# First attention step of a sigmoid-attention plus ReLU² feed-forward kernel: half of its scores moved to two-part products, its first queries loaded and multiplied in halves, three warm-up matmuls fewer

## The chip, the cores and the metric

One core of a Trainium2 chip runs the whole program. The metric is device time in microseconds (us), the median of a few runs; lower is better. The engines are PE (TensorE, with PEld for its weight loads), DVE (VectorE), ACT (ScalarE), POOL (GpSimd) and SP (SyncE, which here only issues transfers). ACT issues transfers too, on a queue of its own.

## The reference, cut to what matters

```
q, k, v: 8 batches x 12 heads x 448 x 64, fp32
attn = sigmoid(q @ k^T / sqrt(64) - log(448))
x    = (attn @ v), heads side by side: 3584 tokens x 768
h    = max(x @ w_in, 0)                # 768 -> 2048
out  = (s * h * h + b) @ w_out         # 2048 -> 768
```

The change touches only the first few microseconds of the attention.

## The kernel before, in words

The heads are worked through four at a time: one *step* takes a tile `qk` of 128 partitions x [2 pairs][queries, keys][448] (two pairs of heads; in a pair, one head lies on partitions 0 to 63 and the other on 64 to 127). There are 24 steps (8 batches x 3), and after them comes the feed-forward part, which is nearly four fifths of the time. The order of all instructions is the order in which the code is written (`manual_schedule`), so each engine works through its list in that order.

A step (the loop `for n, (b, t) in enumerate(quads)`, L584 to L611):

- `scores` (L397): for pair `i` and chunk `c` of 128 keys, both heads' scores go into one bank tile `psc` of 128 x 2 x 448. Steps 1 to 23 (`TWO`, L53) multiply *two parts*: each operand is split as a high part `qkh` rounded to fp32r (a copy) and the rest `qkl` (a subtraction), and three fp32r products (L413) stand for one fp32 product. Step 0 multiplies the raw fp32 operands (L419); one such instruction appears in the trace as two records, so a chunk of step 0 (two heads) is 4 records, a chunk of the other steps 6.
- the scores run through `sigmoid` (L392, on ACT) into a tile `a`; a chunk's bank is free again once its sigmoid is done. Score banks come from a pool of 3 (`ps_qk`); the chunk (0, 2) uses the bank tile of the products with `v` (`ps_av`) instead. In step 0 the warm-up tile `idle` takes the first of the three, so the chunks (0, 0), (0, 1), (1, 0), (1, 1), (1, 2) and the last keys' chunk go round the three banks, and the last keys' chunk waits for the sigmoid of (1, 0).
- `scores_last` (L429): the last 64 keys of both pairs (`psc_l`, L434); that of step n + 1 is run inside step n.
- `parts_hi` (L382, ACT) and `parts_lo` (L388, DVE) split the next step's operands.
- `attn_v` (L440, L445) and `attn_v_last` (L451, L454) multiply with `v` into `pav`; `store_x` (L459) copies the result out and stores it.
- between these, `ticks` runs jobs that prepare the feed-forward weights: raw 64-bit weights are fetched into `st` and converted by DVE and ACT (L204 to L220).

Ahead of the loop: step 0's `qk` tile is loaded in five transfers on two queues (L363 to L367), then step 1's tile as one transfer (L369), `v` of step 0 (L374), two weight tiles `st` (L493) and more, all on SP. PE runs `WARM` matmuls of zeros (L472) until the data are there. ACT loads its table (L467) and makes a small constant `e_bias`, which DVE then overwrites (L468).

In what follows (i, c) is the chunk c of pair i in step 0.

Of the kernel before, what the change touches and what calls it, by code (L numbers as in the profile page):

```python
# [34 lines left out]


TB = 512
WARM = 13
PARTS = ((0, 0), (0, 1), (1, 0))
AHEAD = 6  # L40
PIECES = (2, 1, 1, 2, 1, 1, 2, 1, 1, 2, 1, 1, 2, 1, 1, 2, 1, 1, 2, 1, 2, 1)
# [9 lines left out]
}  # L51
ROLL = 7
TWO = range(1, 24)  # L53

# [40 lines left out]
def sigmoid_attention_relu2_ffn(  # L95
# [10 lines left out]
    nc = tc.nc  # L106
    B, NQ, P, _, _, S = qk.shape
# [44 lines left out]
    first = ExitStack()  # L152
# [23 lines left out]
    def f32(ap):  # L176
        return ap.bitcast(F32)
# [4 lines left out]
    def sub(o, x, y):  # L182
        nc.vector.tensor_tensor(o, x, y, op=ALU.subtract)  # L183
# [170 lines left out]
    ps_av = pool(at, "ps_av", 1, space=PSUM, side="right")  # L354

    half = (slice(0, D), slice(D, P))
    quads = [(b, t) for b in range(B) for t in range(NQ)]
    NL = len(quads)

    def load(b, t, first=False):  # L360
        x = ld.tile([P, 2, 2, S], F32, tag="qk", name=f"qk_{b}_{t}")
        if first:
            nc.sync.dma_start(x[:, 0, 1, :P], qk[b, t][:, 0, 1, :P])  # L363
            nc.scalar.dma_start(x[:, 0, 0], qk[b, t][:, 0, 0])
            nc.sync.dma_start(x[:, 0, 1, P:], qk[b, t][:, 0, 1, P:])
            nc.scalar.dma_start(x[:, 1, 0], qk[b, t][:, 1, 0])
            nc.sync.dma_start(x[:, 1, 1], qk[b, t][:, 1, 1])  # L367
        else:
            nc.sync.dma_start(x, qk[b, t])  # L369
        return [x]  # L370
# [8 lines left out]
    def flat(x):  # L379
        return x.rearrange("p i x s -> p i (x s)")[:, :, :NX]  # L380

    def parts_hi(b, t, ld_):  # L382

        hi, lo = (hl.tile([P, 2, NX], F32R, tag=h, name=f"qk{h}_{b}_{t}") for h in "hl")
        nc.scalar.copy(hi, flat(ld_[0]))
        ld_.append((hi, lo))

    def parts_lo(ld_):  # L388
        hi, lo = ld_[-1]
        sub(lo, flat(ld_[0]), f32(hi))  # L390

    def sigmoid(psc, name):  # L392
        a = ap_.tile([P, 2, S], F32, tag="a", name=f"a_{name}")
        nc.scalar.activation(a, psc[:, :, :S], AF.Sigmoid, bias=nls, scale=SCALE)  # L394
        return a

    def scores(b, t, ld_):  # L397
        x = ld_[0]
        two = ld_.pop() if len(ld_) > 2 else None
        a = {}  # L400
        psc = {}
        order = [(i, c) for i in range(2) for c in range(3)]
        if two:
            order[2:4] = order[3], order[2]
        for i, c in order:

            pl, tag = (ps_av, "pav") if (i, c) == (0, 2) else (ps_qk, "psc")
            o = psc[i, c] = pl.tile([P, 2, 512], F32, tag=tag, name=f"psc_{b}_{t}_{i}_{c}")
            if two:
                cols = slice(S + c * P, S + (c + 1) * P)  # L410
                for m, (wi, xi) in enumerate(PARTS):
                    for j, r in enumerate(half):
                        nc.tensor.matmul(  # L413
                            o[:, j, :S], two[wi][r, i, cols], two[xi][r, i, :S],
                            start=m == 0, stop=m == 2,
                        )
            else:
                for j, r in enumerate(half):
                    nc.tensor.matmul(  # L419
                        o[:, j, :S], x[r, i, 1, c * P : (c + 1) * P], x[r, i, 0, :],  # L420
                        start=True, stop=True,
                    )
            if two and i + c == 1 and i:
                continue
            for k in [(i, c)] + [(1, 0)] * (two is not None and (i, c) == (0, 2)):
                a[k] = sigmoid(psc[k], f"{b}_{t}_{k[0]}_{k[1]}")
        return a

# [35 lines left out]
    loaded = {0: load(*quads[0], first=True)}  # L464
# [18 lines left out]
    def ticks(n, part):  # L483
        for _, _, fn in sorted(plan.pop((n, part), ()), key=lambda x: x[:2]):
            fn()
# [96 lines left out]
    at_step(NL - 1, "DVE", 1, lambda: base(0, 0, w1[0]))  # L582

    for n, (b, t) in enumerate(quads):  # L584
        ticks(n, "DVE")
        a = scores(b, t, loaded[n])
        if n == 0:
            al = scores_last(b, t, loaded[0])
        if n + 1 in TWO:
            parts_hi(*quads[n + 1], loaded[n + 1])  # L590
        ticks(n, "ACT")
        if n + 2 < NL:
            loaded[n + 2] = load(*quads[n + 2])
        ticks(n, "SP")
        for fn in stores:
            fn()
        stores.clear()
        if n == NL - 1:
            qkx.close()
            ps_h = pool(blk_ps, "ps_h", 2, space=PSUM)  # L600
        pav = attn_v(b, t, loaded[n], a)
        last = al
        if n + 1 < NL:
            al = scores_last(*quads[n + 1], loaded[n + 1])
        attn_v_last(loaded[n], last, pav)
        if n + 1 in TWO:
            parts_lo(loaded[n + 1])
        ticks(n, "END")
        store_x(b, t, pav)
        if n + 2 < NL:  # L610
            load_v(*quads[n + 2], loaded[n + 2])  # L611
# [142 lines left out]
    start = [(0, 0), (2, 0), (2, 1), (2, 2), (0, 2), (0, 1), (1, 1), (1, 2), (1, 0)]  # L754
# [4 lines left out]
    for i, f in enumerate(order):  # L759
# [17 lines left out]
        j, stage = divmod(i - LATE_AT, LATE_FOR)  # L777
# [152 lines left out]
    for n, blocks in enumerate(threes):  # L930
# [128 lines left out]
        for u, (i, p) in enumerate(L1):  # L1059
# [10 lines left out]
            for j in range(2):  # L1070
                m = 0
                for c in range(KC):
                    for wi, xi in PARTS:
                        nc.tensor.matmul(  # L1074
                            bk[:, j], wt[:, j, wi, c * P : (c + 1) * P], opd[i][xi][:, c, :],
                            start=i == ch[0] and m == 0,
                            stop=m == 3 * KC - 1,
# [111 lines left out]
        for j, (i, p) in enumerate(L2):  # L1189
# [8 lines left out]
            for e, tk in LAST if end else [(e, slice(TB)) for e in range(KC)]:  # L1198
                o = bk[:, e]
                if end:  # L1200
                    o = ps.tile([P, 2, TB], F32, tag="b", name=f"o_{e}_{tk.start}")[:, 0, tk]
                for f in range(2):
                    for m, (wi, gi) in enumerate(PARTS):
# [3 lines left out]
                            stop=p == NPP - 1 and f == 1 and m == 2,  # L1207
# [61 lines left out]
```

## Time and profile before

| | |
|---|---|
| median of 3 runs | 1039.72 us (1039.62 to 1039.72) |
| the profiled execution's own time | 1039.4 us |
| its span | 1037.5 us |
| PE busy in the span | 1033.5 us |
| DVE, ACT busy | 832.7 us, 618.3 us |
| instructions | 13890 |

The profiled execution takes 1.9 us more than its span (start and end lie outside it). The page of the profile gives busy times, the chain of work that ended last and the costliest groups of instructions; the trace behind it can be asked for every instruction in order of time, for who waited for whom, and for transfers with their time from issue to landing. A PE record's duration reaches over the next record's start, since matmuls are pipelined; how fast PE goes is read from the distance between starts.

### The profile page before, as it was taken

The page shows a single profiled execution, that of the slowest core. Times are in us where ns is not written, and L with a number is a line of the kernel's source. Part 1 is how long each engine was busy: PE and PEld are TensorE (multiplying, and loading weights), DVE is VectorE, ACT ScalarE, POOL GpSimd, SP SyncE. Part 2 cuts the span into 40 slices and gives each one's busy share as a digit, 9 for nine tenths or more (in the row PEclk, how much of TensorE's full clock was granted, in tenths as well). Part 3 has the DMA queues.
Part 4 walks back from the last instruction along what each step waited for, and adds up shares of the span by engine and source line. Part 5 has one row for each costly group of instructions (what it writes and reads, how often), then busy time and mean ns, then how long its engine had stood idle before and what let it go on. Part 6 is the DMA issues. An engine that isn't in the chain of part 4 may idle for free.

```text
span 1037.5 us, 13890 instructions
## 1 busy us (share of the span) xinstructions
PE 1033.5 (100%) x5287; PEld 780.6 (75%) x5287; DVE 832.7 (80%) x900; ACT 618.3 (60%) x667; POOL 0.2 (0%) x4
## 2 busy tenths in 40 slices
PE   9999999999999999999999999999999999999998
PEld 4545555555888888888888888888888888888887
DVE  4999999995988965898898897796455789888777
ACT  7999999988776755574445344344445335552432
POOL 0000000000000000000000000000000000000000
PEclk9999999999999999999999999999999999999999
DMA  8788989995999999999686676897666666676763
GB/s 325 273 333 337 354 325 395 344 397 193 333 364 367 357 408 410 342 342 320 201 269 190 217 229 220 290 318 249 197 192 194 194 193 195 192 228 217 221 228 118
DMA packets 101569, 287.16 MB, mean 277 GB/s; under 512 B 10241, under 2 KB 20353, under 8 KB 101505
## 3 DMA queue, kind: packets, MB, share of 16 engines
q1 hardware_dynamic: 101216, 285.84, 79.2%
q8 instruction: 42, 0.69, 0.3%
q10 hardware_dynamic: 288, 0.46, 0.1%
q14 instruction: 23, 0.18, 0.0%
HBM read 198.18 MB, written 88.08 MB: 276 GB/s over the span
## 4 chain that ended last, share of the span: by engine, by line
PE 100%; DVE 0%; issue 0%
PE o L1204 31%; PE h L1074 31%; PE pav L445 11%; PE psc L413 9%; PE ph L553 6%; PE po L744 6%; PE psc_l L434 2%; PE pav L454 2%; PE psc L419 1%; PE idle L472 0%; DVE C_t L183 0%; DVE zero L165 0%; DVE nls L166 0%
## 5 line engine op out<-in xcount | busy, mean ns | idle before, releaser
L1074 PE MATMUL h<-s_1h,wu 128*128 128x512 f32 x480 | 148.0, 389 | 0.0
L1074 PE MATMUL h<-s_0h,wu 128*128 128x512 f32 x480 | 147.8, 389 | 0.0
L394 ACT ACTIVATE a<-psc,nls 128x896 f32<-128x896 f32 x144 | 132.7, 1009 | 12.9 <-PE psc L413 10.2
L445 PE MATMUL pav<-a,v 128*64 128x448 f32 x576 | 113.5, 543 | 0.0
L1074 PEld LDWEIGHTS h<-s_1h,wu 128*128 128x128 f32 x480 | 90.1, 188 | 18.8
L1074 PEld LDWEIGHTS h<-s_0h,wu 128*128 128x128 f32 x480 | 90.1, 188 | 18.6
L947 ACT COPY G<-h 128x1024 f32<-128x1024 f32 x48 | 48.9, 1018 | 85.0 <-PE h L1074 58.0
L839 ACT ACTIVATE G<-G,b_sb,s_sb 128x1024 f32<-128x1024 f32 x48 | 59.8, 1245 | 61.4 <-DVE G L836 60.7
L1074 PE MATMUL h<-s_0l,wu 128*128 128x512 f32 x240 | 93.4, 389 | 0.0
L1074 PE MATMUL h<-s_1l,wu 128*128 128x512 f32 x240 | 93.4, 389 | 0.0
L445 PEld LDWEIGHTS pav<-a,v 128*64 128x64 f32 x576 | 39.2, 137 | 64.0 <-issue 44.8
L180 DVE TENSOR_TENSOR G<-G,h 128x1024 f32<-128x1024 f32 x40 | 48.7, 1219 | 39.0 <-PE h L1074 38.9
L1204 PE MATMUL o<-g_3h,wu 128*128 128x512 f32 (+1 forms) x244 | 79.0, 385 | 0.0
L1204 PE MATMUL o<-g_0h,wu 128*128 128x512 f32 x240 | 78.8, 389 | 0.0
L1204 PE MATMUL o<-g_1h,wu 128*128 128x512 f32 x240 | 78.8, 389 | 0.0
L1204 PE MATMUL o<-g_2h,wu 128*128 128x512 f32 x240 | 78.8, 389 | 0.0
L744 PE MATMUL po<-g,w 128*128 128x512 f32 x288 | 67.7, 389 | 0.0
L744 PEld LDWEIGHTS po<-g,w 128*128 128x128 f32 x288 | 54.1, 188 | 11.2
L553 PE MATMUL ph<-x0h,w 128*128 128x512 f32 x192 | 61.7, 390 | 0.0
L413 PE MATMUL psc<-qkh 64*128 64x448 f32 x276 | 53.0, 380 | 0.0
L1204 PEld LDWEIGHTS o<-g_3h,wu 128*128 128x128 f32 x244 | 45.7, 188 | 9.3
L1074 PEld LDWEIGHTS h<-s_0l,wu 128*128 128x128 f32 x240 | 45.0, 188 | 9.4
(152 smaller groups left out, 2025.4 us busy)
## 6 DMA issues: line engine op xcount, KB each, us to landing
wu<-wd SPq DMA_DIRECT2D x240, 512.0 KB, 4.3
wd<-t SPq DMA_DIRECT2D x36, 768.0 KB, 8.0
qk<-qk_t SPq DMA_DIRECT2D x23, 896.0 KB, 7.2
st<-w_out SPq DMA_DIRECT2D x16, 768.0 KB, 9.3
st<-w_in SPq DMA_DIRECT2D x16, 768.0 KB, 9.5
wd<-w SPq DMA_DIRECT2D x16, 768.0 KB, 5.8
v<-v_t SPq DMA_DIRECT2D x24, 448.0 KB, 5.6
xd<-xo SPq DMA_DIRECT2D x24, 448.0 KB, 4.3
```

The source lines that it names most:

```text
L180: nc.vector.tensor_tensor(o, x, y, op=ALU.add)
L394: nc.scalar.activation(a, psc[:, :, :S], AF.Sigmoid, bias=nls, scale=SCALE)
L413: nc.tensor.matmul(o[:, j, :S], two[wi][r, i, cols], two[xi][r, i, :S], start=m == 0, stop=m == 2,)
L434: nc.tensor.matmul(psc[half[i], j, :S], x[r, i, 1, 3 * P :], x[r, i, 0, :], start=True, stop=True,)
L445: nc.tensor.matmul(pav[r, i, :S], ld_[1][:, 3 * i + c, j, :], a[i, c][:, j, :], start=c == 0, stop=False,)
L454: nc.tensor.matmul(pav[r, i, :S], ld_[1][half[i], 6, j, :], a[half[i], j, :], start=False, stop=True,)
L553: nc.tensor.matmul(ph, w[:, k, wi, kc * P : (kc + 1) * P], x0[h][xi][:, cc, :], start=m == 0, stop=m == 3 * NCC - 1,)
L744: nc.tensor.matmul(pos[e], w[:, k, wi, kc * P : (kc + 1) * P], g[:, gi, :], start=first and i == 0, stop=last and i == 2,)
L839: nc.scalar.activation(x, x, AF.Identity, bias=b_sb, scale=s_sb)
L947: nc.scalar.copy(g(m, h), bk)
L1074: nc.tensor.matmul(bk[:, j], wt[:, j, wi, c * P : (c + 1) * P], opd[i][xi][:, c, :], start=i == ch[0] and m == 0, stop=m == 3 * KC - 1, sk ...
L1204: nc.tensor.matmul(o, wt[:, f, wi, e * P : (e + 1) * P], g[gi][:, f, tk], start=(end or i == ch[0] and p == 0) and f == 0 and m == 0, stop ...
```

## The change

Five things change, all but the last in step 0:

1. `WARM` goes from 13 to 10.
2. The first loads change queues: keys of (0, 0) and the remaining keys of pair 0 go to ACT's queue, the queries of pair 0 to SP's queue in two halves of 224 columns, and the queries of pair 1 stay on ACT's queue, now third there.
3. Chunk (0, 0) is multiplied by halves of the queries (224 columns, four instructions in place of two).
4. Pair 1 of step 0 is multiplied in two parts like the other steps; its parts are made by DVE alone: a copy (`qkh`) and a subtraction (`qkl`) of 128 x 832, ahead of step 0's other DVE jobs.
5. `TWO` is gone: every step has parts. Step 0 keeps its order of chunks.

```diff
-WARM = 13
+WARM = 10
...
+    cols2 = (slice(0, S // 2), slice(S // 2, S))
...
         if first:
-            nc.sync.dma_start(x[:, 0, 1, :P], qk[b, t][:, 0, 1, :P])
-            nc.scalar.dma_start(x[:, 0, 0], qk[b, t][:, 0, 0])
-            nc.sync.dma_start(x[:, 0, 1, P:], qk[b, t][:, 0, 1, P:])
+            nc.scalar.dma_start(x[:, 0, 1, :P], qk[b, t][:, 0, 1, :P])
+            for h in cols2:
+                nc.sync.dma_start(x[:, 0, 0, h], qk[b, t][:, 0, 0, h])
+            nc.scalar.dma_start(x[:, 0, 1, P:], qk[b, t][:, 0, 1, P:])
             nc.scalar.dma_start(x[:, 1, 0], qk[b, t][:, 1, 0])
             nc.sync.dma_start(x[:, 1, 1], qk[b, t][:, 1, 1])
...
-    def parts_hi(b, t, ld_):
+    def parts_hi(n, pairs=slice(0, 2)):
 
+        ld_ = loaded[n]
+        b, t = quads[n]
         hi, lo = (hl.tile([P, 2, NX], F32R, tag=h, name=f"qk{h}_{b}_{t}") for h in "hl")
-        nc.scalar.copy(hi, flat(ld_[0]))
+        copy = nc.scalar.copy if n else nc.vector.tensor_copy
+        copy(hi[:, pairs], flat(ld_[0])[:, pairs])
         ld_.append((hi, lo))
 
-    def parts_lo(ld_):
+    def parts_lo(n, pairs=slice(0, 2)):
+        ld_ = loaded[n]
         hi, lo = ld_[-1]
-        sub(lo, flat(ld_[0]), f32(hi))
+        sub(lo[:, pairs], flat(ld_[0])[:, pairs], f32(hi[:, pairs]))
...
-            if two:
+            if i or not first:
                 cols = slice(S + c * P, S + (c + 1) * P)
...
             else:
-                for j, r in enumerate(half):
-                    nc.tensor.matmul(
-                        o[:, j, :S], x[r, i, 1, c * P : (c + 1) * P], x[r, i, 0, :],
-                        start=True, stop=True,
-                    )
...
+                for s_ in cols2 if (i, c) == (0, 0) else (slice(0, S),):
+                    for j, r in enumerate(half):
+                        nc.tensor.matmul(
+                            o[:, j, s_], x[r, i, 1, c * P : (c + 1) * P], x[r, i, 0, s_],
+                            start=True, stop=True,
+                        )
...
     for n, (b, t) in enumerate(quads):
+        if n == 0:
+            parts_hi(0, slice(1, 2))
+            parts_lo(0, slice(1, 2))
         ticks(n, "DVE")
-        a = scores(b, t, loaded[n])
+        a = scores(b, t, loaded[n], first=n == 0)
```

PE's list where the warm-up ends, before (`psc_0_0_0` is the bank tile of chunk (0, 0), `psc_0_1_0` that of (1, 0); `qk_0` is step 0's tile, a name DMAHW is a transfer's signal):

```order
L472 MATMUL idle<-zero 128x256
L419 MATMUL psc_0_0_0_192<-qk_0_156 128x448 [waits DMAHW1_49,DMAHW0_49]
L419 MATMUL psc_0_0_0_192<-qk_0_156 128x448
L419 MATMUL psc_0_0_1_197<-qk_0_156 128x448 [waits DMAHW2_49]
L419 MATMUL psc_0_0_1_197<-qk_0_156 128x448
L419 MATMUL psc_0_0_2_202<-qk_0_156 128x448 x2
L419 MATMUL psc_0_1_0_207<-qk_0_156 128x448 [waits DMAHW4_49,DMAHW3_49,PE_49]
L419 MATMUL psc_0_1_0_207<-qk_0_156 128x448
L419 MATMUL psc_0_1_1_212<-qk_0_156 128x448 [waits Activation_49]
```

and the same place of the changed kernel:

```order
L479 MATMUL idle<-zero 128x256
L426 MATMUL psc_0_0_0_194<-qk_0_156 128x224 [waits DMAHW1_49,DMAHW0_49]
L426 MATMUL psc_0_0_0_194<-qk_0_156 128x224
L426 MATMUL psc_0_0_0_194<-qk_0_156 128x224 [waits DMAHW3_49]
L426 MATMUL psc_0_0_0_194<-qk_0_156 128x224
L426 MATMUL psc_0_0_1_201<-qk_0_156 128x448 [waits DMAHW2_49]
L426 MATMUL psc_0_0_1_201<-qk_0_156 128x448
L426 MATMUL psc_0_0_2_206<-qk_0_156 128x448 x2
L418 MATMUL psc_0_1_0_211<-qkh_0_188 128x448 [waits DVE_49,PE_49]
L418 MATMUL psc_0_1_0_211<-qkh_0_188 128x448
L418 MATMUL psc_0_1_0_211<-qkl_0_189,qkh_0_188 128x448 [waits DVE_49]
L418 MATMUL psc_0_1_0_211<-qkl_0_189,qkh_0_188 128x448
```

Chunk (0, 0) now waits for two transfers first and for a third half way, and chunk (1, 0) waits for DVE in place of the transfers.

DVE's list at the start of the changed kernel (`st` are raw weights, `qkl_1` is the low part for step 1):

```order
L475 MEMSET e_bias 128x1 [waits Activation_49]
L389 CAST qkh_0_188<-qk_0_156 128x832 [waits DMAHW5_49,DMAHW4_49]
L182 TENSOR_TENSOR qkl_0_189<-qk_0_156,qkh_0_188 128x832 [waits DVE_49]
L203 TENSOR_SCALAR wf_0_105<-st_0_180 128x768 [waits DMAHW0_49]
L203 TENSOR_SCALAR wf_8_107<-st_8_182 128x768 [waits DMAHW1_49]
L182 TENSOR_TENSOR qkl_1_246<-qk_1_163,qkh_1_245 128x1664 [waits DMAHW6_49,PE_49,Activation_49]
```

The second and third row are new; the others follow each other there as before. Behind step 0 no engine's list changes. On SP the first `v` and step 1's tile keep their places (fourth and fifth issue); since eight signals go round the transfers and there is one transfer more, the first `st` fetch now waits for the landing of the first keys, and the second for that of the first half of the queries.

## Rows read from the trace of the kernel before

**Rows 1.** The page: busy times, and the chain that ended last by engine

```profile
PE 1033.5 (100%) x5287; PEld 780.6 (75%) x5287; DVE 832.7 (80%) x900; ACT 618.3 (60%) x667; POOL 0.2 (0%) x4
...
PE 100%; DVE 0%; issue 0%
```

**Rows 2.** Chain that ended last, in order of time: start us, us, what

```profile
1.05 2.95 PE idle L472 x13
4.00 5.64 PE psc L419 x24
9.64 0.94 PE psc_l L434 x8
10.58 4.66 PE pav L445 x24
15.24 0.91 PE psc_l L434 x8
...
16.91 3.90 PE psc L413 x36
...
27.14 3.84 PE psc L413 x36
...
37.33 3.84 PE psc L413 x36
```

**Rows 3.** PE in order of time, 3 to 11 us: start, busy, what

```profile
2.73 1.27 PE L472 MATMUL idle<-zero 128*128 128x256 bf16 x5
```

**Rows 4.** PEld in order of time, 3 to 11 us; in brackets idle time before, releaser

```profile
3.93 0.51 PEld L419 LDWEIGHTS psc<-qk 64*128 64x128 f32 x4 [0.41 <-DMA qk<-qk_t]
4.84 0.34 PEld L419 LDWEIGHTS psc<-qk 64*128 64x128 f32 x2 [0.41 <-issue]
5.59 0.32 PEld L419 LDWEIGHTS psc<-qk 64*128 64x128 f32 x2 [0.41 <-issue]
6.09 0.19 PEld L419 LDWEIGHTS psc<-qk 64*128 64x128 f32 x2 [0.19 <-issue]
6.47 0.19 PEld L419 LDWEIGHTS psc<-qk 64*128 64x128 f32 x2 [0.19 <-issue]
...
9.60 0.21 PEld L434 LDWEIGHTS psc_l<-qk 64*64 64x64 f32 x8 [0.68 <-ACT a L394]
10.51 0.20 PEld L445 LDWEIGHTS pav<-a,v 128*64 128x64 f32 x4 [0.70 <-DMA v<-v_t]
```

**Rows 5.** Stretches 3.9 to 5.5 and 5.5 to 9.5 us: busy, then granted clock, DMA

```profile
3.90:5.50 1.60, 1.60 (x5) 0.85 (x6) 0.00 (x0) 0.00 (x0) 0.00 (x0) 1.00 1.08 310
5.50:9.50 4.00, 4.00 (x22) 1.84 (x18) 0.00 (x0) 3.65 (x5) 0.00 (x0) 1.00 0.93 350
```

**Rows 6.** ACT in order of time, 3 to 18 us

```profile
5.84 5.50 ACT L394 ACTIVATE a<-psc,nls 128x896 f32<-128x896 f32 x6 [2.70 <-PE psc L419]
11.20 1.04 ACT L394 ACTIVATE a_l<-psc_l,nls 128x896 f32<-128x896 f32 x1
```

**Rows 7.** Transfers issued in the first 14 us: KB each, median us to landing

```profile
qk<-qk_t ACTq DMA_DIRECT2D x2, 224.0 KB, 3.1
qk<-qk_t SPq DMA_DIRECT2D x1, 224.0 KB, 3.8
qk<-qk_t SPq DMA_DIRECT2D x1, 160.0 KB, 3.0
qk<-qk_t SPq DMA_DIRECT2D x1, 64.0 KB, 2.6
```

**Rows 8.** Line L364, the first transfer of queries, up to 10 us

```profile
DMA to landing us min/median/max: 2.9/2.9/2.9
```

**Rows 9.** Issue times in order of time, first 6 us

```profile
0.72 0.41 ACTq L364 DMA_DIRECT2D qk<-qk_t  x1
...
1.17 0.45 ACTq L366 DMA_DIRECT2D qk<-qk_t  x1
1.64 0.42 SPq L367 DMA_DIRECT2D qk<-qk_t  x1
1.65 1.28 ACT L467 ACT_TABLE_LOAD   x1 [1.65 <-PEq L1259]
...
2.58 0.43 SPq L374 DMA_DIRECT2D v<-v_t  x1
...
3.05 0.93 SPq L493 DMA_DIRECT2D st<-w_out  x2
```

**Rows 10.** Line L374, issues up to 10 us: transfers of v (steps 0 and 1)

```profile
DMA to landing us min/median/max: 7.5/9.2/11.0
```

**Rows 11.** DVE in order of time, first 30 us

```profile
3.21 0.06 DVE L468 MEMSET e_bias<- 128x1 f32 x1 [2.21 <-ACT e_bias L467]
11.98 0.57 DVE L204 TENSOR_SCALAR wf<-st 128x768 int32<-128x768 int32 x1 [8.71 <-DMA st<-w_out]
13.83 0.56 DVE L204 TENSOR_SCALAR wf<-st 128x768 int32<-128x768 int32 x1 [1.28 <-DMA st<-w_out]
14.32 1.87 DVE L183 TENSOR_TENSOR qkl<-qk,qkh 128x1664 fp32r<-128x1664 f32 x1
16.98 1.09 DVE L461 COPY xo<-pav 128x896 f32<-128x896 f32 x1 [0.79 <-PE pav L454]
```

More of the change, by code (lines that the diff above doesn't have):

```diff
@@ L52 @@
 ROLL = 7
-TWO = range(1, 24)
 SUMS = (
@@ L395, in sigmoid, with scores @@
         return a
-    def scores(b, t, ld_):
+    def scores(b, t, ld_, first=False):
         x = ld_[0]
-        two = ld_.pop() if len(ld_) > 2 else None
+        two = ld_.pop()
         a = {}
@@ L402, in scores @@
         order = [(i, c) for i in range(2) for c in range(3)]
-        if two:
+        if not first:
             order[2:4] = order[3], order[2]
@@ L408, in scores @@
             o = psc[i, c] = pl.tile([P, 2, 512], F32, tag=tag, name=f"psc_{b}_{t}_{i}_{c}")
-            if two:
+            if i or not first:
                 cols = slice(S + c * P, S + (c + 1) * P)
@@ L417, in scores @@
             else:
-                for j, r in enumerate(half):
-                    nc.tensor.matmul(
-                        o[:, j, :S], x[r, i, 1, c * P : (c + 1) * P], x[r, i, 0, :],
-                        start=True, stop=True,
-                    )
-            if two and i + c == 1 and i:
+                for s_ in cols2 if (i, c) == (0, 0) else (slice(0, S),):
[4 more added lines that the diff above has]
+                        )
+            if not first and i + c == 1 and i:
                 continue
-            for k in [(i, c)] + [(1, 0)] * (two is not None and (i, c) == (0, 2)):
+            for k in [(i, c)] + [(1, 0)] * (not first and (i, c) == (0, 2)):
                 a[k] = sigmoid(psc[k], f"{b}_{t}_{k[0]}_{k[1]}")
@@ L584, in sigmoid_attention_relu2_ffn @@
     for n, (b, t) in enumerate(quads):
+        if n == 0:
+            parts_hi(0, slice(1, 2))
+            parts_lo(0, slice(1, 2))
         ticks(n, "DVE")
-        a = scores(b, t, loaded[n])
+        a = scores(b, t, loaded[n], first=n == 0)
         if n == 0:
             al = scores_last(b, t, loaded[0])
-        if n + 1 in TWO:
-            parts_hi(*quads[n + 1], loaded[n + 1])
+        if n + 1 < NL:
+            parts_hi(n + 1)
         ticks(n, "ACT")
@@ L605, in sigmoid_attention_relu2_ffn @@
         attn_v_last(loaded[n], last, pav)
-        if n + 1 in TWO:
-            parts_lo(loaded[n + 1])
+        if n + 1 < NL:
+            parts_lo(n + 1)
         ticks(n, "END")
```

## The prediction

> **What bounds the kernel now.** I read the page first: PE is busy for 1033.5 of 1037.5 us and the chain that ended last is all PE [rows 1]. The chain in order of time says more [rows 2]: the scores of steps 2 and 3 begin at 27.14 and 37.33 us, 10.19 us apart, with PE products end to end. So whatever step 0 gains or loses goes through to the end undiminished, as long as the suppliers of step 1 are early enough; and nothing else in the program changes. Only the first 10 us need looking at.
>
> Under the lens they read as follows. Warm-up matmuls run from 1.05 us to 4.00, the last five in 1.27 us [rows 2, 3]; with a last record of about 0.42 us that is one per 0.21 us. Then PE works in pairs of records (both heads at once), and the weight loads show their pace [rows 4]: a load starts some 0.09 us after the pair ahead of its own, so pairs start at 4.00, 4.75, 5.50, 6.00, 6.38. That is 0.75 us a pair, once 0.50, then 0.375 us, the two levels of TensorE's clock (1.2 and 2.4 GHz); the column of the granted clock shows 1.00 for both stretches [rows 5] and doesn't tell them apart. The third pair, 0.50 us long, puts the rise at about 5.75 us, after warm-up and pairs with no long break. ACT starts its first sigmoid at 5.84, 0.34 us after the first chunk's end at 5.50, and does six in 5.50 us, so one per 0.90 us and 1.00 for the last [rows 6]. PE at full clock needs 0.75 us for a chunk, so ACT is the slower one: the last keys' chunk waits at 9.60 for the sigmoid of (1, 0) [rows 4], which starts at 5.84 + 3 x 0.90 = 8.54 and ends at 9.54. **PE feels ACT there**, and only there.
>
> **The change, part by part.**
>
> *Three warm-ups fewer, other queues.* The warm-up ends 3 x 0.21 = 0.63 us sooner, at 3.37. When are the data there? Before, the 64 KB of keys landed 2.6 us after issue [rows 7] and the 224 KB of queries 2.9 us after it [rows 8], at 3.33 and 3.6 [rows 9]. Now the first product needs 64 + 112 KB in place of 288: bounds 3.33 and 3.6, and I take 3.4, near the smaller transfer. Was the first load at 3.93 held by the data or by the tail of the warm-up? It is put down to the transfer, but that had landed 0.3 us earlier; and it starts 0.07 us before the end of the matmuls ahead of it (4.00), as the load of the next part does (10.51 against 10.58) [rows 2, 4]. I take the tail: first product at about 3.45, 0.55 sooner. If 0.3 us are a latency, it is 3.7, and with the data as late as before 4.0, no gain at all.
>
> *Chunk (0, 0) in halves.* Four pairs of 224 columns at 0.37 us, cold; their loads take about 0.33 us [rows 4] and fit under them: the same 1.49 us, nothing added; at worst some 0.05 us a pair. The second half of the queries, in the slot in which 160 KB took 3.0 us from 1.17 [rows 7, 9], lands by 4.17; it is wanted at 4.2. Covered by the first half, barely.
>
> *The clock takes half of it back.* If the rise stays at 5.75, the earlier start is spent cold. (0, 0) ends at 3.45 + 1.49 = 4.94, its sigmoid starts at 5.28. (0, 1): one pair to 5.69, 0.06 us more cold, the rest at full clock, end 6.09 (before 6.38). Its sigmoid can't start before 6.43, so ACT, free at 6.18, waits: 0.31 us are left of 0.55. Then one sigmoid per 0.90: (0, 2) 7.33, (1, 0) 8.23 to 9.23.
>
> *Two-part scores of pair 1.* Six pieces a step take 3.84 us [rows 2], 0.64 a chunk against 0.75: 3 x 0.11 = 0.33 us of PE. I cost the gain at **nothing**: what hides it is ACT, since the last keys' chunk can't start before 9.23 + 0.06 whatever PE does. Without ACT in the way the 0.33 would come on top.
>
> *The parts on DVE.* DVE has no work from 3.27 to 11.98 us [rows 11], so nothing queues behind them; the `st` conversion waits for its transfer anyhow. They need the queries and keys of pair 1. Before, the last of the five landed at 1.64 + 3.8 = 5.44 [rows 7, 9]; the bytes are the same, so I take 5.4 for both. Subtraction: half of the row of 1664 elements, 0.95 us. The copy has no row of its own: conversions of 768 elements take 0.57, a copy of 896 out of PSUM 1.09 [rows 11], by size 0.6 to 1.0; I take 0.6, both operands being in SBUF as in the first. With 0.1 for signals the low part is there at 7.05, 7.45 with the slow copy. PE reaches (1, 0) at 6.84, wants the low part 0.2 later and must end by 8.23 - 0.34 = 7.89, so the low part may come as late as 7.4: covered, in the slow case 0.05 us short, which would take 0.05 us off the sum. A rule bears on the copy: the Trainium skill, "VectorE: DVE Perf Modes" (the perf-mode tier table), gives 1.23 us for an fp32 copy of 2048 elements between SBUF tiles, twice the pace that PSUM operands get. Cut by size that is an estimate of 0.5 us, by which the sum stays as it is; no run here shows it yet.
>
> *Queues.* ACT issues one transfer more, 0.45 us, so its table load starts at 2.1 and ends at 3.4, with `e_bias` behind it by 3.6; the first sigmoid comes at 5.28: hidden. On SP, step 1's tile and `v` keep their slots. The `st` fetches are issued some 0.3 us later than at 3.05, behind a `v` that lands only at 2.58 + 7.5 = 10.08 [rows 9, 10]: hidden by that backlog.
>
> *What is late next.* The products with `v` began loading at 10.51 and would at 10.2; `v` at 10.08 allows 0.4 us of gain, no more. In step 1 the low part is done at 16.19 [rows 11], tied to the second `st` at 13.83; PE wants it 0.2 us after 16.91, now after 16.6: covered.
>
> **Sum.** Last keys' chunk at 9.32 in place of 9.64: minus 0.3 us, rounded. Against the profiled execution 1039.4 - 0.3 = 1039.1; the median of the runs shown is 0.3 us above that one, so **1039.4** for the median. A change under 0.2% (2.1 us) can't be told from none by the measurement, so this is "same".
>
> **The rivals.**
>
> 1. *The clock rises later* (slower). Place: chunks (0, 1) to (1, 2). With ten warm-ups PE stands still from 3.2 or 3.4 us until the data are there, up to 0.6 us, where before it hardly did. Each us that the rise is late costs half a us; at 6.4 the gain is gone. If it comes only at the end of the scores, these take 6 pairs x 0.75 cold plus 9 x 0.37 (one pass in place of two), from 3.45 to 11.3: 1.65 us lost, 1041.4. For it: the gap. Against: the gap is short, and three runs within 0.10 us say that the rise comes at the same place each time. The Trainium skill, "TensorE: Matmul & The Clock Gate" (Part 1), says that the rise wanders by half a microsecond from run to run and that activity alone releases the full clock; by the first, the time would scatter by 0.25 us, which the runs shown don't do; the second speaks for this rival. 10%.
> 2. *The parts come late.* Queries of pair 1 are third on ACT's queue and may share the transfer engines with step 1's 896 KB. The turning point against before is the low part at 7.8 us (then the sigmoid of (1, 0) starts at 8.55 as before), a landing at 6.1, or 5.75 with the slow copy; beyond, each tenth costs a tenth. A landing at 6.6: 0.5 us slower, 1040.2. Against: both queues carry 448 KB of the first tile now as before. 12%.
> 3. *Nothing comes out*: first product at 3.7 to 4.0 (latency or late data), or `v` lands 0.3 us later and holds PE. 1039.6 to 1039.8. 15%.
> 4. *More comes out*: the rise moves forward with the work, `v` comes earlier too: 0.55 us or somewhat more, 1039.1 or less. 6%.
>
> **How the numbers follow.** The forecast has 57%: a gain of 0.2 to 0.5 us, 1039.2 to 1039.6. The range takes in rivals 3 and 2 and the first half of 1, and on the low side most of 4: 1039.0 to 1040.3. To be faster by over 2.1 us more warm-up and scores would have to vanish than the 0.63 + 0.33 + 0.25 (ACT's wait) there are: 1%. Slower by over 2.1 us needs the clock to stay low beyond the first scores: 3%. The rest, 96%, is within 0.2%.
>
> **What would show it.** Right: the first load at 3.4 and a first sigmoid at about 5.3, the second one after a wait, loads 0.75 and 0.375 us apart with the change at about 5.75, PE waiting for ACT ahead of the last keys' chunk at about 9.3, then the same spacings to the end. Wrong: loads 0.75 us apart beyond 6.4; DVE's new rows ending after 7.4 and PE's load of (1, 0) waiting for DVE; PE waiting for `v`; the steps after it no longer 10.19 us apart.

## The result, and the profile after

The change is **slower**: 1042.23 us median of 22 runs (1039.79 to 1044.72) against 1039.38 of the kernel before (22 runs, 1038.78 to 1040.43); ratio 1.0025, interval 1.0019 to 1.0031. That is 0.25%, clear of the noise; the forecast was 1039.4 and "same". The runs of the change fall into two groups. Twelve have a mean granted clock of 1.0 and a median of 1040.5; ten have 0.997 or 0.998 and a median of 1043.6. None of the hundred or so runs of the kernel before that ran beside the experiments lies at 0.997 or 0.998. The plain median, 1042.23, lies between the medians of the two groups. Two executions far off all others, one of the kernel before (1750.92 us, clock 0.556) and one of an experiment (1298.6 us, clock 0.753), are left out of the ratios.

The first profiled execution is one of the first group (1040.92 us). Its page gives the span (1037.5 us before):

```profile
span 1038.7 us, 13910 instructions
```

The chain in order of time (start, length, what), against [rows 2]:

```profile
1.17 3.49 DMA qk<-qk_t
4.66 0.04 issue
4.70 4.13 PE psc L426 x12
8.83 0.02 issue
8.85 1.91 ACT a L399 x2
10.77 0.04 issue
10.81 1.08 PE psc_l L441 x8
```

The last keys' chunk starts at 10.81 in place of 9.60 [rows 4]; from there to the span's end it is 1027.9 us both times. So the span's loss of 1.2 us lies wholly ahead of this point (a further 0.3 us of the time lies outside the span: 2.2 us in place of 1.9). In the profiles of the experiments this remainder is 1027.8 to 1028.3 us, apart from two that are named below, so the start of this chunk can stand for the time. PEld in order of time (start, busy, idle time before it), against [rows 4]:

```profile
3.30 0.51 PEld L426 LDWEIGHTS psc<-qk 64*128 64x128 f32 x4 [0.42 <-DMA qk<-qk_t]
4.70 1.25 PEld L426 LDWEIGHTS psc<-qk 64*128 64x128 f32 x8 [0.90 <-DMA qk<-qk_t]
6.36 0.34 PEld L426 LDWEIGHTS psc<-qk 64*128 64x128 f32 x2 [0.41 <-issue]
7.10 0.34 PEld L426 LDWEIGHTS psc<-qk 64*128 64x128 f32 x2 [0.41 <-issue]
7.85 0.34 PEld L418 LDWEIGHTS psc<-qkh 64*128 64x128 f32 x2 [0.41 <-issue]
8.60 0.26 PEld L418 LDWEIGHTS psc<-qkl,qkh 64*128 64x128 f32 x2 [0.41 <-issue]
8.87 0.18 PEld L418 LDWEIGHTS psc<-qkh,qkl 64*128 64x128 f32 x2
9.07 0.19 PEld L418 LDWEIGHTS psc<-qkh 64*128 64x128 f32 x2
```

The first load is at 3.30, as forecast. Then two things are wrong. PE waits for the second half of the queries, which lands at 4.66 and not by 4.17; and the loads stay 0.75 us apart until 8.60, so the clock rises at about 8.65 and not 5.75. DVE, against [rows 11]:

```profile
6.28 0.59 DVE L389 CAST qkh<-qk 128x832 fp32r<-128x832 f32 x1 [2.53 <-DMA qk<-qk_t]
6.91 1.02 DVE L182 TENSOR_TENSOR qkl<-qk,qkh 128x832 fp32r<-128x832 f32 x1
```

Pair 1's operands landed at 6.25 and not 5.4, but in this execution PE was so late itself that it didn't wait for the parts. One execution doesn't tell the cause; the experiments are fourteen further kernels and three more executions of the change.

### The profile page after: what moved, and what is told of

Same layout as the page of the kernel before. It is cut to its first block, busy times and chain, and to the rows that moved or that the text cites. A ratio compares the mean times of both kernels' runs of the same rounds, so it can differ in the third digit from the quotient of the medians.

```text
span 1038.7 us, 13910 instructions
## 1 busy us (share of the span) xinstructions
PE 1034.2 (100%) x5294; PEld 781.9 (75%) x5294; DVE 834.6 (80%) x902; ACT 618.4 (60%) x667; POOL 0.2 (0%) x4
## 4 chain that ended last, share of the span: by engine, by line
PE 99%; DMA 0%; ACT 0%; DVE 0%; SPq 0%; issue 0%
PE o L1214 31%; PE h L1084 31%; PE pav L452 11%; PE psc L418 9%; PE ph L560 6%; PE po L754 6%; PE psc_l L441 2%; PE pav L461 2%; PE psc L426 0%; DMA qk<-qk_t 0%; ACT a L399 0%; DVE C_t L182 0%; SPq L365 0%
## 5 line engine op out<-in xcount | busy, mean ns | idle before, releaser
L1214 PEld LDWEIGHTS o<-g_1h,wu 128*128 128x128 f32 x240 | 45.1, 188 | 9.4
```

What stands on the lines that cost most here:

```text
L1214: nc.tensor.matmul(o, wt[:, f, wi, e * P : (e + 1) * P], g[gi][:, f, tk], start=(end or i == ch[0] and p == 0) and f == 0 and m == 0, stop ...
```

## The experiments

A run's "landing" is below the time at which the later of pair 1's two transfers is there; "clock" is the mean granted clock of a run. Each group below has its own runs of the kernel before: medians 1039.67, 1039.67, 1039.24 and 1039.52 us for the groups 1 to 4, and one run of 1039.09 us for group 5. A ratio is that to the kernel before, with its 95% interval in brackets.

### 1. The clock's rise, the warm-up or the parts?

**The change with 13 warm-ups** (`WARM = 10` → `13`).

> The changed kernel with 13 warm-up matmuls in place of 10, all else as changed. Clock theory (the loss comes from PE standing still between the two halves of chunk (0, 0), 4.0 to 4.7 us, after which the full clock comes some us later): with 13 the first half starts at 4.0 and ends at 4.75, when the second half of the queries has just landed (4.67), so there is no standstill; loads go from 0.75 to 0.375 us apart at about 5.8 us, time about 1039.4. Parts theory (the loss comes from pair 1's two-part scores and their making on DVE): about 1042. Transfer theory (the second half of the queries lands late and that costs by itself): about 1042, since it lands no sooner.

Measured: 1041.54 us, 1.0020 (1.0010 to 1.0029); 4 of 11 runs have a clock of 0.998. In its profile PE doesn't wait between the halves and the clock has risen by 5.6, yet the time is lost: pair 1's operands land at 7.86 (issue 1.64, 6.2 us). DVE and PEld:

```profile
7.89 0.59 DVE L389 CAST qkh<-qk 128x832 fp32r<-128x832 f32 x1 [4.14 <-DMA qk<-qk_t]
```

```profile
6.06 0.19 PEld L426 LDWEIGHTS psc<-qk 64*128 64x128 f32 x2 [0.19 <-issue]
8.60 0.22 PEld L418 LDWEIGHTS psc<-qkh 64*128 64x128 f32 x2 [2.35 <-issue]
9.60 0.18 PEld L418 LDWEIGHTS psc<-qkl,qkh 64*128 64x128 f32 x2 [0.78 <-DVE qkl L182]
...
11.41 0.27 PEld L441 LDWEIGHTS psc_l<-qk 64*64 64x64 f32 x8 [0.30 <-ACT a L399]
```

PE stands still for the copy (load at 8.60), then for the subtraction (9.60). A late rise of the clock is not needed for the loss.

**Zeros between the halves**, to keep PE busy there:

```diff
+                    if s_.start:
+                        for _ in range(3):
+                            nc.tensor.matmul(idle[:, 0, : 2 * P], zero[:, :P], zero, start=True, stop=True)
```

> The changed kernel with three matmuls of zeros between the two halves of chunk (0, 0), 0.64 us of PE where it stood still for 0.66 us; 10 warm-ups as changed. Clock theory: the second half starts at 4.70 to 4.75 as before, but the clock rises at about 5.8 us: about 1039.3. Warm-up theory (it is the smaller number of warm-ups that delays the clock): stays near 1042 less a little. Parts theory and transfer theory: about 1042.

Measured: 1042.31 us, 1.0027 (1.0015 to 1.0038); 1 of 6 runs at 0.998. The clock has risen by about 5.5 in its profile, but the landing is at 8.58 and the last keys' chunk starts at 12.13. The gap between the halves isn't the cause of the median. PE's loads stand still longer here than in any other profile at 1.0:

```profile
9.32 0.21 PEld L418 LDWEIGHTS psc<-qkh 64*128 64x128 f32 x2 [2.69 <-issue]
```

**The kernel before with 10 warm-ups** (`WARM = 13` → `10`).

> The kernel before with 10 warm-ups in place of 13, nothing else. PE stands still from 3.4 to about 3.6 us, until the queries land. Clock theory: a standstill of 0.2 to 0.3 us matters little, the first product comes 0.3 us sooner: 1039.0 to 1039.6, spread of the runs as before (about 1.6 us). Warm-up theory: about 1041 to 1042, with runs as far apart as those of the changed kernel (4.9 us).

Measured: 1039.85 us, 1.0002 (0.9993 to 1.0011), no run below 1.0. Fewer warm-ups alone change nothing that the runs can show. In its profile pair 1's keys land at 6.8 against 5.4 before [rows 7, 9], although the transfers are the same: the landing scatters.

**The parts alone** (the change, with 13 warm-ups and with the loads and the whole first chunk of before).

```diff
+            nc.sync.dma_start(x[:, 0, 1, :P], qk[b, t][:, 0, 1, :P])
+            nc.scalar.dma_start(x[:, 0, 0], qk[b, t][:, 0, 0])
+            nc.sync.dma_start(x[:, 0, 1, P:], qk[b, t][:, 0, 1, P:])
...
-                for s_ in cols2 if (i, c) == (0, 0) else (slice(0, S),):
+                for s_ in (slice(0, S),):
```

> The changed kernel with 13 warm-ups and the loads and the whole chunk (0, 0) as before: what is left of the change is pair 1 in two parts made by DVE. Clock theory: no standstill of PE, the gain hidden behind ACT: 1039.1 to 1039.5, equal to before. Parts theory: about 1042. Transfer theory: 1039.4.

Measured: 1040.28 us, 1.0006 (0.9997 to 1.0015), no run below 1.0. Landing at 6.26; PE waits for the low part, and the last keys' chunk starts at 9.87:

```profile
8.05 0.19 PEld L417 LDWEIGHTS psc<-qkl,qkh 64*128 64x128 f32 x2 [0.78 <-DVE qkl L182]
```

### 2. Why do pair 1's operands land late?

**Queries of pair 1 on SP's queue, ahead of pair 1's keys.**

```diff
-            nc.scalar.dma_start(x[:, 1, 0], qk[b, t][:, 1, 0])
+            nc.sync.dma_start(x[:, 1, 0], qk[b, t][:, 1, 0])
```

> The changed kernel with the queries of pair 1 on SP's queue, between the second half of pair 0's queries and the keys of pair 1, so ahead of step 1's tile in the same queue; ACT's queue has only keys of pair 0. Turns theory (the last rows of the queries of pair 1, on ACT's queue, take turns with the 7168-byte rows of step 1's tile on SP's queue and land late, by a time that differs from run to run; the low part is ready 1.7 us after that landing, and time goes up by what the landing is later than about 5.7 us): queries and keys land at 5.5 to 6.5 us, 1039.4 to 1040.4, no run above 1042. Clock theory (the standstill between the halves, which stays here): 1041 to 1042. Bytes theory (pair 1 is simply too many bytes too early): no change, about 1042.

Measured: 1041.50 us, 1.0019 (1.0010 to 1.0028), 1 of 11 runs at 0.998. The 1040.4 of the turns theory was missed. The profile is of the 0.998 run (1043.05): the landing is at 7.84 on one queue too, and the last keys' chunk starts at 12.87.

**The same transfer behind step 1's tile** (issued on SP between that tile and `v`).

```diff
-            nc.scalar.dma_start(x[:, 1, 0], qk[b, t][:, 1, 0])
...
     loaded[1] = load(*quads[1])
+    nc.sync.dma_start(loaded[0][0][:, 1, 0], qk[0, 0][:, 1, 0])
     load_v(*quads[0], loaded[0])
```

> The suspected cost doubled: the queries of pair 1 on SP's queue behind step 1's tile. Turns theory, by the landing alone: they land at 9 to 9.5 us, the low part is ready at about 11, time about 1039.3 + 3.5 = 1042.8, and with PE standing still for over 3 us the clock falls, so that runs of 1043 to 1045 with a mean granted clock of 0.998 are the rule; runs closer together than those of the changed kernel. Clock theory (standstill between the halves alone): as the changed kernel, 1042 and 4.9 us of spread.

Measured: 1045.88 us, 1.0057 (1.0043 to 1.0072), all 5 runs at 0.997 or 0.998. Landing at 10.56, last keys' chunk at 15.66. A later landing drives the time, and it brings the lower clock every time.

**The loads, halves and warm-up of the change without the parts** (pair 1 as fp32 products).

```diff
-        two = ld_.pop()
+        two = None if first else ld_.pop()
...
-            if i or not first:
+            if not first:
```

> The changed kernel's loads, halves and 10 warm-ups, but pair 1 of step 0 multiplied in fp32 as before, no parts in step 0. Turns theory: the landing is as late as in the changed kernel, but PE needs it 1.7 us later (no copy and subtraction behind it), at about 7.2 us: part of the runs lose, median 1039.6 to 1041. Parts theory: 1039.4, spread as before. Clock theory: about 1041.5 to 1042.

Measured: 1040.05 us, 1.0004 (0.9995 to 1.0013). With the parts-only kernel this makes a table of two by two: neither 1039.67, parts alone 1040.28, loads alone 1040.05, both 1041.54 (13 warm-ups) to 1042.23. **By the medians, the two together cost more than the sum of both (0.6 + 0.4)**; neither alone is clear of the noise, and neither alone has a run at 0.997 or 0.998 (0 of 22), where the two together have 14 of 33. The profile of this kernel, at 1038.68 us, also shows what caps the gain when all goes well: the last keys' chunk is at 8.69, and then PE waits for `v`:

```profile
8.69 0.21 PEld L441 LDWEIGHTS psc_l<-qk 64*64 64x64 f32 x8 [0.65 <-ACT a L399]
9.81 0.20 PEld L452 LDWEIGHTS pav<-a,v 128*64 128x64 f32 x4 [0.91 <-DMA v<-v_t]
```

**The change with step 1's tile in four transfers**, so that its rows are 1792 bytes long like pair 1's, not 7168.

```diff
+        elif (b, t) == (0, 1):
+            for i in range(2):
+                for k in range(2):
+                    nc.sync.dma_start(x[:, i, k], qk[b, t][:, i, k])
```

> The changed kernel with step 1's tile loaded in four transfers of 1792-byte rows in place of one with 7168-byte rows; queues and the rest as changed. Turns theory: a turn of the other queue takes a quarter of the time, so the last rows of the queries of pair 1 land 1 to 2 us sooner, at 5.5 to 6.5 us; median 1039.5 to 1040.5, hardly a run with a lower mean granted clock. Bytes theory: no change, about 1042. Clock theory: no change.

Measured: 1040.84 us, 1.0012 (1.0003 to 1.0021), none of 11 runs below 1.0. Landing at 6.91, last keys' chunk at 10.45. What is queued behind pair 1 bears on the loss; about half of it is gone.

### 3. Taking the competitor away

**The change with everything on SP behind pair 1's keys held until the copy is done** (a one-element write into `v`'s tile on DVE, for which `v`'s transfer waits).

```diff
+    parts_hi(0, slice(1, 2))
+    held = loaded[0].pop()
+    vt = ldv.tile([P, 7, 2, D], F32, tag="v", name="v_0_0")
+    nc.vector.memset(vt[:1, 0, 0, :1], 0.0)
+    nc.sync.dma_start(vt, v[0, 0])
+    loaded[0].append(vt)
+    loaded[0].append(held)
     loaded[1] = load(*quads[1])
-    load_v(*quads[0], loaded[0])
```

> The change, with `v` of step 0, step 1's tile and every later transfer on SyncE's queue held back until VectorE has copied pair 1's high part. Landing theory (the last rows of pair 1 lag because step 1's tile, with rows twice as long, shares the DMA engines with them): pair 1's operands land at 4.8 to 5.4 us instead of 6.25 to 8.6, the copy starts by 5.5, the low part is ready by 7.2, there is no standstill before pair 1's products, no run has a mean granted clock below 1.0, and the last keys' chunk starts at 9.3 to 9.8. But `v` then lands at 9 to 10 and step 1's tile late, which costs up to about 1 us in step 1: 1040 to 1041 us in all, against 1042.2 of the change. Byte theory (the rows lag because of what the two queues carry ahead of them, whatever follows): landings stay at 6.2 to 8.6 us, 1042 or more.

Measured: 1040.59 us, 1.0012 (1.0003 to 1.0021). Its ten runs lie within 0.62 us (1040.25 to 1040.87), where the change's spread over 4.9; none is below 1.0. The copy starts at 5.89, somewhat later than the landing theory had it, the last keys' chunk at 9.66. What remains is the price of the hold, in step 1, as expected (18.30; from the last keys' chunk to the span's end it is 1029.1 us here):

```profile
7.60 0.19 PEld L418 LDWEIGHTS psc<-qkl,qkh 64*128 64x128 f32 x2 [0.30 <-DVE qkl L182]
...
9.66 0.30 PEld L441 LDWEIGHTS psc_l<-qk 64*64 64x64 f32 x8 [0.54 <-ACT a L399]
...
18.30 0.18 PEld L418 LDWEIGHTS psc<-qkl,qkh 64*128 64x128 f32 x2 [1.13 <-DVE qkl L182]
```

With nothing queued behind pair 1, the landing is at 5.87 in the profile, and the scatter of the time and the lower clock are gone.

**Before with 10 warm-ups and the tile in four transfers** (`WARM = 10` and the four-transfer edit above).

> The kernel before with 10 warm-up products instead of 13 and step 1's tile in four transfers with rows of 1792 bytes; no parts. Landing theory: pair 1's keys land at about 5.4 us instead of the 6.84 seen with 10 warm-ups and the whole tile, and the time is 1039.3 to 1039.8 us. Byte theory: landing and time as with 10 warm-ups and the whole tile, 1039.85 us.

Measured: 1039.89 us, 1.0006 (0.9997 to 1.0015). The keys land at 5.44 as the landing theory has it, but the time is that of the whole tile (1039.85), just above its bound. Without parts PE needs pair 1 only at some 6.8 us; an earlier landing buys nothing.

**The change's loads without parts, the tile in four transfers.**

> The change's loads, halves and 10 warm-ups, pair 1 as fp32 products without parts, and step 1's tile in four transfers with rows of 1792 bytes. Landing theory: pair 1's operands are there before 6.9 us as in the small-row run of the change, and without the 1.7 us of copy and subtraction that is before they are needed, so no standstill: 1039.2 to 1039.8 us, the gain capped by `v`, which lands at 9.8 or later. Parts theory (the parts alone cost, the loads nothing): the same as the loads without parts and the whole tile, 1040.05 us.

Measured: 1039.66 us, 1.0004 (0.9995 to 1.0013), as the landing theory has it; landing at 6.2, last keys' chunk at 8.90, and PE goes on with `v` at 9.81 as above (so 1028.6 us remain from that chunk on).

### 4. The clock, and a better order

**Zeros on PE ahead of pair 1's first product and ahead of its low part**, with the landing as it is.

```diff
+                    if first and (i, c) == (1, 0) and m < 2:
+                        for _ in range((12, 8)[m]):
+                            nc.tensor.matmul(o[:, 0, : 2 * P], zero[:, :P], zero, start=m == 0, stop=m == 0)
```

> The change plus products with zeros on TensorE ahead of pair 1's first product (12 of 256 columns, 1.3 us at full clock) and ahead of its low part (8, 0.86 us). They add nothing to the sums. Clock-fall theory (about half of the change's runs lose a further 3 us because the granted clock falls while PE stands still): no run has a mean granted clock below 1.0, the highest run is at 1042 or less and the median at 1040.2 to 1041.0, that of the change's undisturbed runs; operands still land at 6.2 to 8.6 us. Rival (the runs at 0.998 come from later landings alone, the clock being only a sign of them): runs between 1042.9 and 1044.7 stay, median 1041.5 to 1042.5.

Measured: 1041.61 us, 1.0020 (1.0011 to 1.0029). None of 11 runs is below 1.0, against 10 of 22, but median and highest run (1043.52) are above the expected: the zeros ran later than meant. In the profile the first twelve start only as the copy ends (8.78) and stand in pair 1's way:

```profile
8.81 1.21 PEld L419 LDWEIGHTS <-zero 128*128 128x128 bf16 x12 [1.22 <-issue]
10.23 0.19 PEld L421 LDWEIGHTS psc<-qkh 64*128 64x128 f32 x2 [0.21 <-issue]
10.63 0.77 PEld L419 LDWEIGHTS <-zero 128*128 128x128 bf16 x8 [0.22 <-issue]
11.61 0.19 PEld L421 LDWEIGHTS psc<-qkl,qkh 64*128 64x128 f32 x2 [0.21 <-issue]
```

The low part was ready at 9.85 and used at 11.61, so some 1.7 us are the zeros' own. That the lower clock comes of a standstill of PE is borne out; how long a standstill brings it, and what it costs, this run doesn't give.

**The change with `v` ahead of step 1's tile** (the two calls in the other order; `v` has rows of 3584 bytes).

```diff
-    loaded[1] = load(*quads[1])
     load_v(*quads[0], loaded[0])
+    loaded[1] = load(*quads[1])
```

> The change with `v` of step 0 (rows of 3584 bytes) ahead of step 1's tile (rows of 7168 bytes) on SyncE's queue. Row-size theory (the rows of the next transfer decide how late pair 1's last rows are): between the change and the run with rows of 1792 bytes: landing at 6.3 to 7.0 us, few or no runs with a clock below 1.0, median 1040.4 to 1041.2. Rival (it is the bytes of the two queues, not what follows): landing and time as in the change, 6.25 to 8.6 us, 1041.5 to 1042.5.

Measured: 1041.01 us, 1.0013 (1.0004 to 1.0022); ten runs between 1039.62 and 1042.60, none of them below 1.0 (the eleventh is the one of 1298.6 us). Landing at 6.1, last keys' chunk at 9.80.

**The same order without parts, the tile in four transfers** (the best guess for a kernel that beats both).

> The change's loads, halves and 10 warm-ups, pair 1 as fp32 products without parts, `v` of step 0 ahead of step 1's tile, that tile in four transfers with rows of 1792 bytes. The loads without parts had the last keys' chunk at 8.69 us, and PE then waited 0.91 us for `v`. Expected with `v` at about 7.5 us instead of 9.8: no wait for `v`, 1038.8 to 1039.5 us, so 0 to 0.6 us below the kernel before. Against it: step 1's tile lands some 2 us later, at about 11 to 12 us, and its copy on ACT (from about 11.2) may wait: then up to 1 us is given back in step 1.

Measured: 1039.91 us, 1.0002 (0.9993 to 1.0011). No wait for `v` in its profile, but no gain: pair 1's operands land at 8.1. Up to and with `v`, this kernel and the one before it issue the same transfers in the same order; yet the queries of pair 1 took, from issue to landing, in the run with parts

```profile
DMA to landing us min/median/max: 4.5/4.5/4.5
```

and in the run without

```profile
DMA to landing us min/median/max: 6.5/6.5/6.5
```

So the landing scatters by 2 us with queues that are equal up to `v` (and by 1.7 us among the four profiles of the change itself), and single profiles don't settle what the row size does. Without parts, too, a landing this late holds PE, but by a whole us less: the last keys' chunk starts 2.55 us after the landing, as it does in the profile of the loads without parts (6.14 and 8.69):

```profile
10.66 0.21 PEld L445 LDWEIGHTS psc_l<-qk 64*64 64x64 f32 x8 [0.65 <-ACT a L403]
```

No kernel tried here beats the one before by more than its interval.

### 5. The change again, unedited

> The change as it is, profiled again. Theory of the falling clock: if this execution is one at 0.997 to 0.998 (1042.9 us or more), pair 1's operands land at 7.5 us or later, TensorE stands still for 2 us or more ahead of pair 1, and the windows from there on show a granted clock of 0.5 for about 3 us; if it is one at 1.0 (1041 us or so), they land earlier or the clock has risen so late that TensorE doesn't wait. Rival (the clock stays low from the start in those runs, rising only after 9 us): no standstill ahead of pair 1, loads 0.75 us apart through all the first step.

> As e16a: the same kernel and the same two readings, a further execution.

> As e16a: the same kernel and the same two readings, a further execution.

Measured: 1043.04 us at a clock of 0.998; 1040.10 and 1040.19 at 1.0. The first is like the group at 0.997 or 0.998. Its DVE and PEld rows, and the windows of 2 us from 6 on (the columns are the engines' busy times, then the granted clock, the share of the DMA engines, GB/s):

```profile
7.95 0.59 DVE L389 CAST qkh<-qk 128x832 fp32r<-128x832 f32 x1 [4.20 <-DMA qk<-qk_t]
8.58 1.03 DVE L182 TENSOR_TENSOR qkl<-qk,qkh 128x832 fp32r<-128x832 f32 x1
```

```profile
6.26 0.19 PEld L426 LDWEIGHTS psc<-qk 64*128 64x128 f32 x2 [0.19 <-issue]
8.66 0.21 PEld L418 LDWEIGHTS psc<-qkh 64*128 64x128 f32 x2 [2.22 <-issue]
9.66 0.29 PEld L418 LDWEIGHTS psc<-qkl,qkh 64*128 64x128 f32 x2 [0.78 <-DVE qkl L182]
9.83 0.34 PEld L418 LDWEIGHTS psc<-qkh,qkl 64*128 64x128 f32 x2
10.21 0.33 PEld L418 LDWEIGHTS psc<-qkh 64*128 64x128 f32 x2
...
12.91 0.21 PEld L441 LDWEIGHTS psc_l<-qk 64*64 64x64 f32 x8 [0.51 <-issue]
```

```profile
6.00:8.00 2.00, 1.17 (x6) 0.26 (x4) 0.05 (x1) 1.81 (x3) 0.00 (x0) 1.00 1.00 352
8.00:10.00 2.00, 0.81 (x4) 0.55 (x6) 1.57 (x2) 0.38 (x1) 0.00 (x0) 0.85 1.01 406
10.00:12.00 2.00, 2.00 (x12) 1.77 (x12) 0.00 (x0) 1.07 (x2) 0.00 (x0) 0.50 0.99 416
12.00:14.00 2.00, 2.00 (x16) 0.74 (x16) 0.56 (x1) 1.92 (x3) 0.00 (x0) 0.80 0.97 381
```

The clock had risen at about 5.9. The operands landed at 7.93, PE stood still, first for the copy, then for the subtraction, and the granted clock fell to 0.50 (1.2 GHz) just as the products began: their loads are 0.37 us apart where they were 0.20. The rival reading, a clock that is low from the start, is out for this execution. Not every such wait brings the clock down: the loads stood still for 2.22 us ahead of the copy here, but for 2.35 with 13 warm-ups and for 2.69 with zeros between the halves, and there the clock stayed up. What decides it is not shown. The second execution, with a landing of 6.45, shows the same waits, shorter, at full clock:

```profile
7.18 0.21 PEld L418 LDWEIGHTS psc<-qkh 64*128 64x128 f32 x2 [0.52 <-PE psc L426]
8.18 0.19 PEld L418 LDWEIGHTS psc<-qkl,qkh 64*128 64x128 f32 x2 [0.78 <-DVE qkl L182]
...
9.99 0.27 PEld L441 LDWEIGHTS psc_l<-qk 64*64 64x64 f32 x8 [0.30 <-ACT a L399]
```

**One sum for most of them.** Where PE waits for the parts, the last keys' chunk starts 3.55 us after the landing: 1.7 for signals, copy and subtraction, the rest PE and one sigmoid.

| kernel | landing | landing + 3.55 | last keys' chunk | over |
|---|---|---|---|---|
| parts alone | 6.26 | 9.81 | 9.87 | 0.06 |
| change, second new profile | 6.45 | 10.00 | 9.99 | 0 |
| tile in four transfers | 6.91 | 10.46 | 10.45 | 0 |
| 13 warm-ups | 7.86 | 11.41 | 11.41 | 0 |
| zeros between the halves | 8.58 | 12.13 | 12.13 | 0 |
| pair 1 on one queue, 0.998 | 7.84 | 11.39 | 12.87 | 1.48 |
| change, first new profile, 0.998 | 7.93 | 11.48 | 12.91 | 1.43 |
| pair 1 behind the tile, 0.997 | 10.56 | 14.11 | 15.66 | 1.55 |
| change, first profile (late rise) | 6.25 | 9.80 | 10.81 | 1.01 |

So a tenth of landing costs a tenth beyond 6.05 (9.60 - 3.55), and a clock that falls meanwhile costs 1.4 to 1.6 us on top, in the three profiles that show it. The other four profiles with parts: the third new one is 0.02 over the sum, `v` ahead of the tile 0.13, the held tile 0.24 (in these two the clock rose only at some 7 us, so that PE itself was late), and the zeros on PE 1.71, their own length.

## Why the prediction was wrong, point by point

- **First product at 3.45: right.** The load is at 3.30. The reading that the tail of the warm-up, not the data, held it stands; so does `v` as the cap of the gain.
- **Second half of the queries by 4.17, "covered, barely": failed in one of four profiles of the change** (4.66); in the other three PE's load for it is at 4.07, 4.11 and 4.21. It took its duration from one row [rows 7] with no margin.
- **"The bytes are the same, so I take 5.4 for both": this is the step that failed.** The landings in the four profiles of the change are 6.25, 6.45, 6.46 and 7.93. Even the kernel before with 10 warm-ups has 6.8: the 5.44 of [rows 7, 9] was one draw from a scatter. The argument "Against" in rival 2 used the same bytes. The deadline itself was in the working (a landing at 6.1); what was left out is that the landing scatters across it. The last keys' chunk follows a late landing by 3.55 us with parts and by 2.55 without, so the parts bring the deadline forward by 1.0 us, to 6.05, and PE now feels a scatter that the products without parts, whose loads take pair 1 at some 6.85, mostly let pass.
- **Rival 2 was the mechanism, right in its arithmetic, too small in its price.** Its turning point, a landing at 6.1, and "each tenth costs a tenth" are what the table shows (6.05). Its price was worked out for a landing of 6.6 (1040.2), where the new profiles at 6.45 have 1040.10 and 1040.19; landings near 8 weren't considered, and 12% was given to what sets the time in three of the four profiles of the change.
- **The clock: two misses.** "The rise stays at 5.75" rested on three runs within 0.10 us. The rise is at about 8.65, 5.9, 6.2 and 7.1 in the four profiles of the change, by the distances of the loads. The rule that was cited from the Trainium skill, "TensorE: Matmul & The Clock Gate" (Part 1), that the rise wanders by half a microsecond from run to run, is borne out, and by more than that: 5.9, 6.2 and 7.1 are from executions in which PE's work up to there started within 0.15 us of each other, and with the same loads without parts the rise is at about 4.0. In the first profile, with its rise at 8.65, this was rival 1's mechanism, without which the parts would have been late there too, by 0.2 us. And no case of the prediction had the clock **fall** again while PE stands still for the data, which costs 1.4 to 1.6 us in the profiles that show it; 10 of the 22 runs have the mean clock of such an execution. The Trainium skill, "TensorE: Matmul & The Clock Gate" (section "HAM oscillation — how this bites in real kernels"), describes the like for a loop of another kernel: a wait for a transfer lets the clock drop, and the next work starts cold; the granted clock of 0.50 from 10 to 12 us agrees.
- **Copy 0.6, subtraction 0.95: nearly right** (0.59; 1.02 to 1.03).
- **The moved queues, ACT's table load, the `st` fetches: no cost seen.** ACT's first sigmoid waits for PE, not for the table (idle before it ended by PE), and step 1's low part is ready at 16.84 in the first profile, where PE starts on step 1's scores at 18.22.
- **The chances.** 96% for "within 0.2%" came from treating the rivals one by one with one value each. They hang together: a late landing makes the wait, and the wait can bring the clock down. The bound for "slower", 2.1 us, is reached by a landing of 7.9 with a fallen clock (3.3 us over before).

Not settled is why the last rows of pair 1 lag by up to 2 us in some executions. That the transfers behind them go on meanwhile is seen: in the first new profile (landing at 7.93), 1.14 MB had been moved by 6 us, more than the 896 KB of the whole first tile, and between 6 and 8 us ACT's queue (q10), which carries only this tile, still had 9 packets, beside 124 of SP's (q1):

```profile
q1 hardware_dynamic: 124, 0.69, 97.4%
q10 hardware_dynamic: 9, 0.01, 3.0%
```

In the second (6.45) ACT's queue had none left by then. With the transfers behind them held, ten runs lie within 0.62 us; with four transfers of short rows, or with `v` next in line, no run of 21 is below 1.0; but one profile with both edits (and no parts) had 8.1. Mostly the queries on ACT's queue and the keys on SP's land within 0.2 us of each other, which gives no sign that the order within one queue is the cause; in the profile with zeros between the halves they land 2.7 us apart.

## What to carry to other kernels

A conversion put between a transfer and its consumer moves the transfer's deadline forward by its own length, less what it saves behind it: here 1.7 us, of which the shorter products gave some 0.7 back. With data in time, the gain was put at nothing. Ahead of such a move, compare the new deadline with the scatter of the landing over several executions, not with one row. And on TensorE price a wait near the start twice: once for its length and once for the clock that may fall in it.

## What was not expected of the hardware

- Equal transfers in equal order landed 4.5 or 6.5 us after issue, in two kernels whose queues differ only behind the next transfer, `v`.
- The granted clock fell from 1.00 to 0.50 (1.2 GHz) after PE had done one pair of products between 7.2 and 9.6 us, and was back at 1.00 by 14; in two other profiles a longer standstill left it at 1.00.
- The rise of the clock, read from the distance between loads, lay between about 4.0 us (the change's loads without parts, whose first sigmoid starts at 4.74) and 8.65 us, though the page shows a granted clock of 1.00 from the start.
